# Spreading V by eight one-pass products in 32x128 tiles, with a new order of the work behind them

## The chip, the core and the metric

The kernel runs on one core of a Trainium2 chip. The metric is the device time of one execution in microseconds (us). Five engines work side by side: PE (TensorE, matrix products), DVE (VectorE), ACT (ScalarE), POOL (GpSimd) and SP (SyncE, which here only starts DMAs). Each engine takes its own instructions in the order in which the program lists them, and waits for the others by semaphores.

## The reference

The first half is a scan over sequences (Mamba-2 style, in chunks), the second a mixer of low rank with two dense layers. What matters here:

```python
# x: (4, 8, 768, 32), a: (4, 8, 768), B and C: (4, 8, 768, 16)
for c in range(seq // 32):                       # chunks
    M = (C_c @ B_c.T) * decay(i, j) * causal     # within a chunk
    y_c = M @ x_c + (C_c @ state) * decay_to_i
    state = decay_full * state + (decay_from_j * B_c).T @ x_c
x = y as (4, 768, 256)
h = (x.T @ U) @ V                                # U: (768, 32), V: (32, 768), over the sequence
u = x + h.T
out = u + relu(u @ w_ch1) @ w_ch2                # (256, 1024), (1024, 256)
```

U, V and the weights arrive as float64, so the kernel makes fp32 of them itself.

## The kernel before

**Tiling.** The sequence is worked on in 12 pairs: 4 batches times 3 stretches of 256 positions. For a pair k the steps have one-letter names: P (B and C times decays, DVE, tile `BC`), T (transposes on PE, copies to `T` and `Cm` by ACT), g (`gram`, products of 32x64 tiles into four banks), m and M (`mask`, DVE, tile `M`), s (`state`, PE) and u (`update`, DVE, tile `S`, with POOL making `Sm`), i and j (`inter`, PE, products of `T` and `Sm`), n (`intra`, PE, products of `x` and `M`), y (`yout`, ACT copies to `yT`), t or O (`ytokens`, PE transposes, a copy to `ytok`).

For a batch b the mixer has p (`project`, the product with U, L685), q (`parted`, which makes `ps`, the product p spread over partitions and its remainder), a (`added`, the product of `Vs` and `ps`, L703, that DVE adds to `yT`; two halves j of 384 positions), and then the two layers: for batch 0 U (`plain`, fp32) and for batches 1 to 3 S, f, e, h, J (`split`, `first`, `second`, `third`, `fourth`), which work with operands split into near, far and both parts in fp32r; and d (`down`, the second layer, in pieces, the last of which adds `Vs` times `ps` and sends the output). In PE's program an fp32 product is two MATMULs, each with a weight load of its own; an fp32r product is one.

**Weights.** They come as 32-bit words. `c` (`convert`, `to_fp32`) is called four times for each of 10 pieces: two operations on DVE and one on ACT, one on ACT, two on DVE, one on DVE. c0 and c2 are the first quarter of `w_ch1` (tile `w1f`), c3 to c5 its other quarters, c6 to c9 the quarters of `w_ch2` (tiles `w2c`), c1 is U and V. `R` (`refine`) splits a quarter for the later batches.

**Order.** There is no automatic scheduling: the string `PLAN` lists the steps word by word, and `follow` issues them in that order, so that each engine's program is the part of the plan that falls to it. Words that begin with b, x, B, X, L, w, W, Z, z start loads on SP; a load under B, X, w or L is held until the last DVE operation that was issued before it. F are products of ones that fill time (`warm`). PSUM has 8 banks that go round, the tag `words` has 15 buffers that go round.

**V.** The word v calls `spread` (L818 to L830). V stands in four strips of 32 partitions in `Vq`. ACT makes `Vn`, V in fp32r; DVE writes the remainder over `Vq` (the tile `UV` in the profile). Then PE copies each of the four strips i to all four strips of bank `v[i]`: for q = 0 to 3 a product with a 32x32 piece of the identity, of Vn for even q, of the remainder for odd q. These are 16 fp32 products in 32x32 tiles (L826). ACT copies the banks to `Vs`. The words behind v are `x4.1 b4.1 b4.2 u3.0 u3.1 p0 c2 n3 c0 P4 c0 i3 q0 c2 b5.2 b5.0 T4 T4 j3 y3.0 y3.1 W2 W3 b5.1 W4 a0.0 c2 c2 a0.1 x4.0 w5`.

Of the kernel before, what the change touches and what calls it, by code (L numbers as in the profile page):

```python
# [10 lines left out]
FP32 = mybir.dt.float32  # L11
INT32 = mybir.dt.int32
UINT32 = mybir.dt.uint32
FP32R = mybir.dt.float32r
WCOLS = 512
NWORDS = 15
# [7 lines left out]
ALU = mybir.AluOpType  # L24
# [52 lines left out]


@with_exitstack
def kernel(  # L80
# [27 lines left out]
    nc = tc.nc  # L108
    P = 128
    NB, NH, S, D = x.shape  # L110
    N = B.shape[-1]
    NC = S // P
    NPR = NC // 2
    DM = NH * D
    RK = moe_U.shape[1]
# [7 lines left out]
    Q = 32  # L123
# [3 lines left out]
    const = ctx.enter_context(tc.tile_pool(name="const", bufs=1))  # L127
    raw = ctx.enter_context(tc.tile_pool(name="raw", bufs=4))
    att = ctx.enter_context(tc.tile_pool(name="att", bufs=2))
# [21 lines left out]
    class Kept:  # L151
# [15 lines left out]
    vector = Kept(nc.vector)  # L167
# [7 lines left out]
        out=a_sb,  # L175
# [43 lines left out]
    Vq = UV[:, 1]  # L219
    Vn = const.tile([P, NC * RK], FP32R)  # L220
    Vs = const.tile([P, S], FP32R)
    w1 = [const.tile([P, NCB, DF], FP32R, name=f"w1{i}") for i in range(3)]
    w1all = mix.tile([P, NQ, NCB, W], FP32, tag="u", name="w1f", bufs=1)
    w1f = [w1all[:, c] for c in range(NQ)]
# [28 lines left out]
    own = {}  # L253
# [39 lines left out]
    ident = const.tile([P, P], FP32)  # L293
# [4 lines left out]
    def triangle(name, out, pattern, base, mult, in_=None):  # L298
        nc.gpsimd.affine_select(
            out=out, in_=ones[:, :out.free_size()] if in_ is None else in_, pattern=pattern,  # L300
            compare_op=ALU.is_ge, fill=0.0, base=base, channel_multiplier=mult)
        return out
# [9 lines left out]
    for v in range(2):  # L312
        half = slice(v * H, v * H + H)
        vector.tensor_tensor(out=ref[half, half], in0=upto[half, half],
                                in1=low[v][half, half], op=ALU.subtract)

    same = const.tile([P, Q], FP32)
# [4 lines left out]
    mine = const.tile([P, NH], FP32)  # L322
    triangle("mine", mine, [[-N, NH]], 0, 1)
    triangle("mine", mine, [[N, NH]], N - 1, -1, in_=mine)
    def warm(n, tag="w"):

        idle(bank(tag, 4 * P), n)
# [6 lines left out]
    for g in range(2):  # L334
# [3 lines left out]
        out=la.rearrange("p b c h -> p b h c"),  # L338
        in0=la_ps.rearrange("p g (b h c) -> p (g b) h c", h=NH, c=NC),
        scalar1=1e-6, scalar2=1.0, op0=ALU.max, op1=ALU.min)  # L340
# [17 lines left out]
    for v in range(2):  # L358
        half = slice(v * H, v * H + H)
        vector.tensor_scalar(out=causal[half], in0=upto[half, half], scalar1=-1.0,  # L360
                                scalar2=None, op0=ALU.mult)
# [20 lines left out]
    def keep(bs, tag="w"):  # L382

        n = bs.stop - bs.start
        d = bank(tag, n, NC, 2, NH)
        nc.tensor.matmul(out=d[:, :, :, 0], lhsT=middle, rhs=la[:, bs], start=True, stop=True,
                         skip_group_check=True)
        for m, sl in ((high, slice(0, NC - 1)), (low[0], slice(1, NC))):
            nc.tensor.matmul(out=d[:, :, :NC - 1, 1], lhsT=m, rhs=la[:, bs, sl], start=False,
                             stop=True, skip_group_check=True)  # L390
        J = 2 * NC - 1
        own = att.tile([P, NB, J, NH], FP32, tag="own", name="own", bufs=1)[:, :n]
        vector.tensor_tensor(
            out=own, in0=d.rearrange("p b c v h -> p b (c v) h")[:, :, :J],
            in1=mine[:, None, None, :].to_broadcast(own.shape), op=ALU.mult)
        vector.tensor_reduce(out=kept[:, bs], in_=own, axis=mybir.AxisListType.X, op=ALU.add)
        nc.scalar.activation(kept[:, bs], kept[:, bs], AF.Exp)
        nc.gpsimd.tensor_tensor(
            out=own2[:, bs], in0=kept[:, bs, :, None].to_broadcast([P, n, J, 2]),
            in1=slot[:, None, None, :].to_broadcast([P, n, J, 2]), op=ALU.mult)  # L400
# [417 lines left out]
    def spread():  # L818

        nc.scalar.copy(out=Vn, in_=Vq)  # L820
        vector.tensor_tensor(out=Vq, in0=Vq, in1=Vn.bitcast(FP32), op=ALU.subtract)
        v = [bank(tag, NC * RK) for tag in "yyxz"]
        for q in range(4):
            for i in range(4):
                rows = ts(i, Q)
                nc.tensor.matmul(out=v[i][ts(q, Q)], lhsT=ident[rows, rows],  # L826
                                 rhs=Vq[rows] if q % 2 else Vn[rows].bitcast(FP32),
                                 start=True, stop=True, skip_group_check=True)
        for i in range(4):
            nc.scalar.copy(out=Vs[:, ts(i, NC * RK)], in_=v[i])  # L830

# [23 lines left out]
    def ytokens_kept(k):  # L855
# [9 lines left out]
                 v=lambda n: spread())  # L865
# [51 lines left out]
```

## Time and profile before

| what | us |
|---|---|
| median of 3 runs | 222.32 |
| lowest and highest | 221.99, 222.81 |
| the profiled execution's own time | 222.37 |
| its span in the profile | 220.7 |

The span runs from the first to the last instruction; the profiled execution's own time is 1.67 us longer. The profile has busy times by engine, and lists instructions with engine, line of the kernel, operation, "written <- read" tiles, shapes and counts. For matrix products it gives the tile (rows * columns of the array) ahead of the shape. In brackets stands how long the engine was idle just before, and what ended that; "issue" means nothing that the profile shows. Matmuls overlap, so their durations add up to more than the time from start to start.

### The profile page before, as it was taken

How to read it: one execution, taken by the hardware profiler on the slowest of the kernel's cores; microseconds unless marked ns; L12 is line 12 of the kernel's file. 1: busy time of each engine (PE TensorE's matmuls, PEld its weight loads, DVE VectorE, ACT ScalarE, POOL GpSimd, SP SyncE). 2: the span in 40 equal slices, each digit the busy share in tenths (PEclk: the TensorE clock that was granted, in tenths of full speed). 3: DMA queues.
4: the chain of work that ended last, by engine and by line, in shares of the span. 5: the costliest groups of instructions: out<-in, count | busy, mean ns of one | idle time of the engine just before them, and what ended most of it. 6: DMA issues, size and time to landing. Idle time of an engine off the chain costs nothing.

```text
span 220.7 us, 7036 instructions
## 1 busy us (share of the span) xinstructions
PE 211.9 (96%) x3012; PEld 181.1 (82%) x3012; DVE 154.5 (70%) x330; ACT 114.3 (52%) x261; POOL 15.5 (7%) x37
## 2 busy tenths in 40 slices
PE   7999889999999999999999999999999999999993
PEld 4657565556578789997999899889989999999993
DVE  4786779899985977475298883973847763729832
ACT  2436856857867353765543237246466446366210
POOL 3021010011001300002000210010000000000000
PEclk9999999999999999999999999999999999999999
DMA  6987779778847070000700000200000100020003
GB/s 89 138 118 153 136 120 328 109 164 216 109 59 118 28 98 24 24 3 9 113 27 1 27 18 30 70 11 3 1 3 0 46 28 0 2 70 3 1 27 115
DMA packets 69518, 14.56 MB, mean 66 GB/s; under 512 B 63792, under 2 KB 67696, under 8 KB 69488
## 3 DMA queue, kind: packets, MB, share of 16 engines
q1 hardware_dynamic: 69488, 14.13, 32.4%
q8 instruction: 23, 0.38, 0.7%
q14 instruction: 7, 0.06, 0.1%
HBM read 10.98 MB, written 3.15 MB: 64 GB/s over the span
## 4 chain that ended last, share of the span: by engine, by line
PE 86%; DVE 6%; ACT 3%; issue 2%; DMA 1%; POOL 0%; DVEq 0%; ACTq 0%; POOLq 0%
PE x L731 29%; PE z L731 24%; PE y L731 12%; PE y L642 3%; PE y L620 2%; PE x L516 2%; PE w L485 2%; DVE words L162 2%; PE w L548 2%; PE w L662 2%; PE z L516 1%; PE w L685 1%; DVE M L162 1%; DVE BC L162 1%; PE w L693 1%
## 5 line engine op out<-in xcount | busy, mean ns | idle before, releaser
L162 DVE SCALAR_TENSOR_TENSOR words<-words 128x768 fp32r<-128x768 f32 (+6 forms) x44 | 33.8, 801 | 2.7 <-ACT words L421 1.0
L731 PE MATMUL x<-u,w 128*128 128x384 f32 x144 | 32.4, 344 | 0.0
L731 PE MATMUL z<-u,w 128*128 128x384 f32 x144 | 32.1, 340 | 0.2 <-DVE words L162 0.2
L731 PEld LDWEIGHTS x<-u,w 128*128 128x128 f32 x144 | 24.5, 188 | 0.4 <-issue 0.2
L731 PEld LDWEIGHTS z<-u,w 128*128 128x128 f32 x144 | 24.3, 188 | 0.6 <-issue 0.5
L731 PE MATMUL x<-w2c,words 128*128 128x256 f32 x112 | 23.2, 339 | 0.0
L736 ACT ACTIVATE x<-x 128x384 f32<-128x384 f32 (+1 forms) x30 | 13.7, 456 | 18.3 <-PE x L731 15.4
L162 DVE SCALAR_TENSOR_TENSOR words<-x,words 128x384 fp32r<-128x384 f32 x24 | 13.1, 552 | 12.8 <-ACT words L765 12.6
L162 DVE SCALAR_TENSOR_TENSOR words<-z,words 128x384 fp32r<-128x384 f32 x24 | 13.0, 551 | 12.8 <-ACT words L765 12.8
L731 PE MATMUL y<-w,words 128*128 128x256 f32 x144 | 20.3, 281 | 0.0
L731 PEld LDWEIGHTS x<-w2c,words 128*128 128x128 f32 x112 | 18.4, 189 | 1.4
L731 PEld LDWEIGHTS y<-w,words 128*128 128x128 f32 x144 | 19.3, 189 | 0.2 <-ACT words L765 0.2
L736 ACT ACTIVATE z<-z 128x384 f32<-128x384 f32 (+1 forms) x27 | 12.5, 464 | 13.2 <-PE z L731 13.2
L765 ACT ACTIVATE words<-z 128x384 fp32r<-128x384 f32 x24 | 11.7, 494 | 8.1 <-PE z L731 7.3
L765 ACT ACTIVATE words<-x 128x384 fp32r<-128x384 f32 x24 | 11.2, 490 | 7.1 <-PE x L731 7.1
L576 POOL TENSOR_TENSOR Sm<-S,own 128x256 f32<-128x256 f32 (+1 forms) x12 | 8.6, 721 | 81.8 <-DVE S L162 63.1
L731 PE MATMUL x<-w,words 128*128 128x256 f32 x96 | 14.1, 284 | 0.0
L731 PEld LDWEIGHTS x<-w,words 128*128 128x128 f32 x96 | 12.8, 188 | 0.3 <-issue 0.2
L162 DVE SCALAR_TENSOR_TENSOR S<-S,kept,w 128x64 f32<-128x64 f32 x40 | 11.2, 280 | 2.4 <-PE w L548 0.4
L731 PE MATMUL z<-yT,w1f 128*128 128x384 f32 x32 | 11.8, 496 | 0.0
L731 PE MATMUL x<-yT,w1f 128*128 128x384 f32 x32 | 11.4, 489 | 0.1
L447 ACT ACTIVATE w<-words 128x512 fp32r<-128x512 f32 x8 | 5.0, 628 | 12.5 <-DVE words L162 12.5
(153 smaller groups left out, 398.5 us busy)
## 6 DMA issues: line engine op xcount, KB each, us to landing
words<-in_moe_w_ch_dram SPq DMA_DIRECT2D x7, 512.0 KB, 5.1
x<-in_x_dram SPq DMA_DIRECT2D x24, 128.0 KB, 3.3
out_dram<-ytok SPq DMA_DIRECT2D x24, 128.0 KB, 1.7
bc<-in_B_dram SPq DMA_DIRECT2D x24, 64.0 KB, 3.0
bc<-in_C_dram SPq DMA_DIRECT2D x12, 128.0 KB, 3.2
words<-in_moe_w_ch_dram SPq DMA_DIRECT2D x2, 256.0 KB, 4.1
words<-in_moe_V_dram SPq DMA_DIRECT2D x4, 48.0 KB, 2.6
words<-in_moe_U_dram SPq DMA_DIRECT2D x1, 192.0 KB, 4.1
```

The source lines that it names most:

```text
L162: self.last = call(*args, **kwargs)
L447: nc.scalar.activation(low, far, AF.Copy, scale=1.0 / EPS)
L485: nc.tensor.transpose(out=tp[:, i, v], in_=s["BC"][:, i, c + v].rearrange("p h n -> p (h n)"), identity=ident)
L516: nc.tensor.matmul(out=g[r][cols, c], lhsT=s["T"][rows, 0, c, cols], rhs=s["Cm"][rows, :, :, ts(2 * c + p, Q)].rearrange("r v t i -> r v i ...
L548: nc.tensor.matmul(out=s["A"][p][ts(r, Q), v], lhsT=s["BC"][half, 0, v, 2 * r:2 * r + 2].rearrange("p h n -> p (h n)"), rhs=x_sb[k][half, ...
L576: nc.gpsimd.tensor_tensor(out=s["Sm"][:, sl], in0=s["S"][:, sl].rearrange("p i (s d) -> p i s d", s=2), in1=own2[:, b, 4 * q:4 * q + sl.st ...
L620: product = nc.tensor.matmul(out=y[p][ts(r % 2, H), r // 2, c], lhsT=own[ts(r, Q)], rhs=s["T"][ts(r, Q), 1, :, ts(2 * c + p, Q)].rearrange ...
L642: product = nc.tensor.matmul(out=y[p][ts(i, Q), n, c], lhsT=x_sb[k][half, c, h], rhs=s["M"][half, h // 2, c, h % 2], start=fresh(k, p, [i] ...
L662: nc.tensor.transpose(out=t[:, c, g], in_=yT[b][:, g, ts(2 * q + c, P)], identity=ident)
L731: nc.tensor.matmul(out=t, lhsT=lhsT, rhs=rhs, start=start, stop=True, skip_group_check=True)
L736: nc.scalar.activation(t, t, AF.Copy, scale=1.0 + EPS)
L765: nc.scalar.activation(gs[j, m // 2][0][:, m % 2], t, AF.Relu, scale=NEAR)
```

## The change

The spread takes 8 products instead of 16. A new constant `sides` (32 rows used at a time, 128 columns) holds the identity of 32 twice, at the even strips for half 0 and at the odd strips for half 1. A product with it copies Vn (half 0) or the remainder (half 1) to two strips at once and writes zeros to the other two; the second product adds to the first. All operands are fp32r, and the remainder has a tile of its own, `Vf`. POOL makes `sides` early on. `own`, a scratch tile of `keep`, takes a buffer of the tag `words` now. All words of the plan behind a0.1 stand in a new order, from `x4.0 w5` on.

```diff
...
-    'W2 W3 b5.1 W4 a0.0 c2 c2 a0.1 x4.0 w5 c3 c3 c3 c3 U0.0.0 P5 U0.0.1 U0.1.1 R0 B6 t3 X5 g4 m4 T5 '
-    'M4 T5 c5 c5 U0.1.0 c5 c5 X6 U0.1.3 c4 c4 s4 u4.0 u4.1 w6 w7 w8 U0.0.3 P6 U0.0.2 c6 U0.0.6 s5 c4 '
-    'c4 U0.1.7 c6 U0.1.2 u5.0 u5.1 R0 L8 T6 c7 U0.1.6 c7 U0.1.5 c7 i4 R3 g5 n4 m5 c6 T6 U0.0.5 M5 c8 '
-    'L7 c8 U0.0.4 c8 c9 c7 U0.1.4 U0.0.7 c9 c9 n5 c6 i5 j4 R5 P8 y4.1 y4.0 P7 g6 j5 m6 L10 y5.1 t4 '
+    'W2 W3 b5.1 W4 a0.0 c2 c2 a0.1 x4.0 w5 c3 c3 c3 X5 g4 c4 w8 c3 t3 w6 U0.0.0 m4 c4 U0.0.1 P5 c4 '
+    'c5 U0.1.0 U0.1.1 c5 w7 B6 U0.1.3 T5 M4 U0.1.2 s4 u4.0 c4 n4 u4.1 s5 c6 R1 R0 c5 L7 u5.0 T5 c9 '
+    'u5.1 c7 U0.0.2 c5 c9 c7 U0.1.5 c7 c6 c6 c6 U0.0.3 U0.0.4 U0.1.4 U0.1.6 c8 P6 c8 U0.0.6 c8 '
+    'U0.1.7 c7 d0.1.2.0 c8 c9 i4 g5 m5 T6 c9 d0.1.2.1 d0.1.2.2 T6 L8 M5 d0.1.2.3 U0.0.5 n5 R0 i5 P7 '
...
-    'h3.1.6 d3.1.0.0 d3.1.0.1 d3.1.0.2 d3.1.1.0 d3.1.0.3 d3.1.1.1 J3.1.0 d3.1.1.2 J3.1.1 J3.1.3 '
-    'd3.1.1.3 J3.1.2 d3.1.2.2 d3.1.2.3 d3.0.1.5 d3.1.0.4 d3.1.1.4 d3.0.0.4 d3.1.0.5 d3.1.2.4 '
-    'd3.1.1.5 d3.1.2.5 d3.0.0.5 d3.0.2.4 d3.0.2.5 ')
+    'e3.1.7 h3.1.7 J3.1.3 d3.1.0.0 J3.1.0 d3.1.1.0 d3.0.0.4 h3.1.5 d3.1.2.1 d3.1.2.2 d3.0.0.5 '
+    'd3.1.1.1 d3.1.0.1 d3.1.0.2 d3.1.0.3 d3.1.2.3 J3.1.2 d3.1.1.2 d3.1.1.3 d3.1.0.4 d3.0.2.4 '
+    'd3.1.2.4 d3.1.1.4 d3.0.1.4 d3.1.1.5 d3.1.2.5 d3.0.1.5 d3.0.2.5 d3.1.0.5 ')
...
+    Vf = const.tile([P, NC * RK], FP32R)
...
+    sides = const.tile([P, 2, 4 * Q], FP32R)
+    for half in range(2):
+        both = sides[:, half].rearrange("p (g s r) -> p s g r", g=2, s=2)
+        for s in range(2):
+            nc.gpsimd.tensor_scalar(
+                out=both[:, s], in0=same[:, None, :].to_broadcast([P, 2, Q]),
+                scalar1=float(s == half), scalar2=None, op0=ALU.mult)
...
-        own = att.tile([P, NB, J, NH], FP32, tag="own", name="own", bufs=1)[:, :n]
+        own = raw.tile([P, 2 * WCOLS], INT32, tag="words", name="words", bufs=NWORDS).bitcast(
+            FP32)[:, :n * J * NH].rearrange("p (b j h) -> p b j h", b=n, h=NH)
...
-        vector.tensor_tensor(out=Vq, in0=Vq, in1=Vn.bitcast(FP32), op=ALU.subtract)
+        vector.tensor_tensor(out=Vf, in0=Vq, in1=Vn.bitcast(FP32), op=ALU.subtract)
         v = [bank(tag, NC * RK) for tag in "yyxz"]
-        for q in range(4):
+        for half, part in enumerate((Vn, Vf)):
             for i in range(4):
                 rows = ts(i, Q)
-                nc.tensor.matmul(out=v[i][ts(q, Q)], lhsT=ident[rows, rows],
-                                 rhs=Vq[rows] if q % 2 else Vn[rows].bitcast(FP32),
-                                 start=True, stop=True, skip_group_check=True)
+                nc.tensor.matmul(out=v[i], lhsT=sides[rows, half], rhs=part[rows],
+                                 start=half == 0, stop=True, skip_group_check=True)
```

56 rows, old and new, of the table PLAN are left out of this document.

## The prediction

> **What bounds the kernel now.** I read the page first, then busy time by stage, then the timeline where the change begins. The page's rows are busy time, granted clock by fortieths, and the chain that ended last by engine:
>
> ```profile
> PE 211.9 (96%) x3012; PEld 181.1 (82%) x3012; DVE 154.5 (70%) x330; ACT 114.3 (52%) x261; POOL 15.5 (7%) x37
> PEclk9999999999999999999999999999999999999999
> PE 86%; DVE 6%; ACT 3%; issue 2%; DMA 1%; POOL 0%; DVEq 0%; ACTq 0%; POOLq 0%
> ```
>
> TensorE (PE) is the bound, at the full clock throughout, and the chain is 86% PE. A busy PE can hide waits, so I look at it by stage (columns: length, then busy us and count of PE, weight loads, DVE, ACT, POOL; clock, DMA share, GB/s):
>
> ```profile
> 28.75:40.00 11.25, 10.62 (x177) 6.88 (x168) 9.90 (x24) 7.75 (x20) 0.95 (x2) 1.00 0.90 229
> 40.00:62.00 22.00, 22.00 (x345) 13.35 (x352) 19.78 (x43) 17.10 (x35) 2.70 (x4) 1.00 0.82 152
> 62.00:100.00 38.00, 37.84 (x613) 32.80 (x599) 28.24 (x60) 20.87 (x46) 3.70 (x7) 1.00 0.27 47
> 100.00:217.00 117.00, 116.82 (x1285) 111.58 (x1283) 76.26 (x138) 55.01 (x126) 3.47 (x7) 1.00 0.10 26
> ```
>
> From 28.75 us on, all that the change reorders, PE is idle for 0.63 + 0 + 0.16 + 0.18 = 0.97 us. A new order of the same work cannot win much more than that from waits. DVE is close behind PE up to 62 us (19.78 of 22.00 us), and far behind it later.
>
> **The spread of V.** This is where the 16 products run, with what stands before and behind them:
>
> ```profile
> 27.14 0.35 PE L826 MATMUL y<-Vn,ident 32*32 32x192 f32 x2
> 27.28 0.35 DVE L162 TENSOR_TENSOR UV<-UV,Vn 128x192 f32<-128x192 f32 x1
> 27.34 0.32 PE L826 MATMUL x<-Vn,ident 32*32 32x192 f32 x1
> ...
> 28.23 0.34 PE L826 MATMUL z<-Vn,ident 32*32 32x192 f32 x1 [0.57 <-issue]
> ...
> 28.50 0.32 PE L826 MATMUL z<-UV,ident 32*32 32x192 f32 x1
> 28.75 0.86 PE L685 MATMUL x<-ytok,UV 128*32 128x256 f32 x16
> 28.91 0.54 ACT L830 CAST Vs<-y 128x192 fp32r<-128x192 f32 x2 [1.82 <-PE z L826]
> ```
>
> Each fp32 product is two MATMULs. Seven of the 32 start by 27.34; then PE stands until 28.23, and the other 25 start within 0.27 us. So of the 1.61 us from the first product to the next work (L685), 0.89 us is a hole between two passes of one product, which no data can explain: the profile calls it "issue". The same word stands twice before it, and I counted what PE did between the holes:
>
> ```profile
> 19.15 0.36 PE L548 MATMUL w<-x,BC 64*32 64x64 f32 x18 [0.27 <-issue]
> 23.15 0.45 PE L642 MATMUL y<-M,x 64*32 64x64 f32 x30 [0.66 <-issue]
> ```
>
> ```profile
> 19.15:23.15 4.00, 3.34 (x127) 2.79 (x127) 3.15 (x10) 2.51 (x7) 0.51 (x1) 1.00 0.66 124
> 23.15:28.23 5.08, 4.23 (x127) 2.76 (x127) 4.26 (x13) 3.59 (x9) 0.18 (x1) 1.00 0.77 137
> ```
>
> ```profile
> q8 instruction: 23, 0.38, 0.7%
> ```
>
> Each time it is 127 matmuls and 127 weight loads, 254 instructions, from hole to hole, and the instruction queue moves 0.38 MB in 23 pieces, 16 KB each. PE waits for the next piece of its own program, at a time when the data DMAs are at 0.66 to 0.77. So I read the hole as one at a fixed place in PE's instruction list, not as one of the spread. Everything ahead of the spread is the same in both programs on PE, so the hole comes behind the same 14 instructions. Before, these are 7 of 32 passes; after, 7 of the 8 one-pass products. Only the eighth is left at 28.23.
>
> [...]
>
> What one product of the new form costs, no row shows (32x128 tile, 192 columns, one pass). The nearest rows bound it: the old passes start some 0.01 us apart (25 in 0.27 us), and full-width one-pass products of 256 columns take 12.76 / 106 = 0.12 us each:
>
> ```profile
> 204.27 12.76 PE y L731 x106
> ```
>
> So 8 take 0.1 to 1.0 us, and I take the dear end, 0.12 each, since the new tiles span all columns. The first four need Vn alone: done by 27.14 + 0.48 = 27.62. The others need Vf from DVE: 27.28 + 0.35 = 27.63, as before. Three end by 28.0, hidden by the hole, and the eighth ends at 28.23 + 0.12 = 28.35. L685 starts there, not at 28.75: **0.40 us** earlier. Bounds: 0 (the piece of program comes later by so much) and 28.75 - 28.17 = 0.58 (no hole: 27.63 + 0.06 + 0.48 = 28.17).
>
> Is it kept? These rows follow:
>
> ```profile
> 30.23 0.68 DVE L162 TENSOR_TENSOR BC<-bc,F 128x512 f32<-128x512 f32 x1
> 31.28 0.60 PE L485 MATMUL w<-ident,BC 128*128 128x128 f32 x4
> 31.48 0.37 ACT L695 CAST ps<-w 128x256 fp32r<-128x256 f32 x1 [0.97 <-PE w L693]
> 31.89 0.43 DVE L162 TENSOR_TENSOR ps<-w,ps 64x256 fp32r<-64x256 f32 x1 [0.64 <-ACT ps L695]
> 32.37 0.45 PE L703 MATMUL x<-Vs,ps 128*128 128x384 f32 x1
> 32.85 0.56 DVE L162 TENSOR_TENSOR yT<-x,yT 128x384 f32<-128x384 f32 x1 [0.54 <-PE x L703]
> ```
>
> Here PE, ACT and DVE wait for each other in turn, and ACT and DVE stand idle before their parts (0.97, 0.64, 0.54), so an earlier PE moves all of it. PE's transposes at 31.28 need BC, ready at 30.91, and can go 0.37 earlier. So all but 0.03 of the 0.40 is kept.
>
> **The rest of the first part.** The subtraction writes Vf, not Vq: the same 0.35 us. Four multiplications for `sides` on POOL, and `own` in a buffer of words:
>
> ```profile
> 3.37 0.19 POOL L299 TENSOR_SCALAR_AFFINE_SELECT mine<-mine 128x8 f32<-128x8 f32 x1
> 9.84 0.37 POOL L398 TENSOR_TENSOR own<-kept,slot 128x88 f32<-128x88 f32 x1 [6.28 <-ACT kept L397]
> ```
>
> POOL idles 6.28 us just where they stand; even at 0.5 us each they cost nothing. If that cover were gone, `own2` would come up to 2 us later (4 x 0.5), and the first Sm behind it. `own` takes a buffer 15 allocations ahead of its next use: nothing.
>
> **The new order.** DVE and ACT issue the same instructions; on PE only their neighbours differ. What neighbours cost:
>
> ```profile
> 149.96 0.86 PE L731 MATMUL z<-u,w 128*128 128x384 f32 x4
> 150.66 0.86 PE L731 MATMUL x<-u,w 128*128 128x384 f32 x4
> 151.44 0.78 PE L620 MATMUL y<-T,Sm 32*64 32x64 f32 x32
> ```
>
> Four products take 0.70 us when products of the same tile follow (149.96 to 150.66), and 0.78 when tiles of 32x64 follow: 0.08 us for a change of tile shape. Counted in the two orders, PE changes shape 70 times before and 66 times after: 4 x 0.08 = **0.3 us** less. Bounds: 0 and, if leaving costs as much again, 0.6.
>
> [...]
>
> Waits: of the 0.97 us of idle PE, some go and some come. I take the sum as unchanged, **0**, since both orders leave DVE and PE about as near to each other at most places; bounds are -0.97 and the DVE rival's +1.65 below. SP issues two loads of x behind an output now, and w2's last quarter ahead of the others; all are due tens of us later.
>
> **The tail.** One product, one addition, one output as before:
>
> ```profile
> 214.22 3.61 SPq L802 DMA_DIRECT2D out_dram<-ytok  x5
> 217.05 0.42 DVE L162 TENSOR_TENSOR ytok<-y,ytok 128x256 f32<-128x256 f32 x1 [0.64 <-PE y L731]
> ```
>
> After, the last five outputs follow at 5 products each, 0.6 us apart; five already go in 3.61 us. Nothing.
>
> **Sum.** The profiled execution took 222.37 us (span 220.7 and 1.67 around it), 0.05 over the median of 222.32. 222.37 - 0.40 - 0.30 = 221.67; on the median's scale **221.6 us**.
>
> **Rivals.**
>
> *DVE sets the pace up to 62 us (slower).* In the new order weights are wanted sooner. From the first addition of V p to the last quarter of w2, DVE has 27.7 us of work and PE 28.1 us before it needs that quarter; before it was 31.6 against 36.7 (counted in the two orders with the mean step of each form). DVE starts 0.48 us behind PE there (32.37 and 32.85 above). The 5 us of reserve are gone. DVE's waits on ACT in this stretch before were:
>
> ```profile
> 42.05 1.31 DVE L162 SCALAR_TENSOR_TENSOR words<-words 128x512 f32<-128x512 f32 x2 [0.71 <-ACT words L421]
> 57.69 1.30 DVE L162 SCALAR_TENSOR_TENSOR words<-words 128x512 f32<-128x512 f32 x2 [0.26 <-ACT words L421]
> 61.54 0.69 DVE L162 SCALAR_TENSOR_TENSOR words<-words 128x512 int32<-128x512 int32 x1 [0.68 <-ACT words L423]
> ```
>
> 0.71 + 0.26 + 0.68 = 1.65 us. If they all come back, PE waits that long, at the down products that read the new quarter: 223.3. Should ACT's conversion steps queue behind relus that wait for PE, one more wait of 0.7 gives 224.0. It is slower than before from 0.7 us of such waits on. For it: the reserve. Against it: ACT is wanted later than DVE in most of the new places, and PE has a wait of its own after the second addition that gives DVE some back. 0.20.
>
> *The waits go (faster).* Between the two additions and the next work PE now has gram and transposes of pairs 4 and 3, where it waited for DVE before; if most of the 0.97 us goes: 220.7 to 221.0. 0.27 for below 221.2.
>
> *The hole goes with the 32 passes.* If it is no wait for a piece of program, L685 starts at 28.17 and the gain there is 0.58: 222.32 - 0.58 - 0.30 = 221.4. For it: the hole lies in a burst of small passes, which are now few. Against it: 254 instructions twice. 0.05. [...]
>
> *The spread gives nothing.* The piece of program comes 0.4 us later, or the hole moves into L685, and its successor at 256 instructions on falls into the next gram: 222.0. 0.13.
>
> **Chances.** Forecast, 221.2 to 221.9: 0.35. About 0.5% (1.1 us) is what a measurement can tell from no change, so faster means below 221.2, slower above 223.4. Faster 0.27. Slower 0.10, half of the DVE rival; its other half lies between 222 and 223.4. Same: 0.35 + 0.05 + 0.13 + 0.10 = 0.63. Range 220.6 to 223.2: it takes in the vanished waits and the DVE rival at most of its price.
>
> **What would show it.** Right: in the timeline a single product of the spread at 28.2 behind "issue", L685 at 28.3 to 28.4, L703 at 32.0, and the same distance to the end less 0.3. Wrong: L685 at 28.7 or later; weight loads or matmuls of the first down products idle on "DVE w2c" or "DVE w1f" between 45 and 62; PE busy in 40 to 62 clearly below its length.

## The result, and the profile after

| | before | after |
|---|---|---|
| median, us (12 runs each, side by side) | 222.26 | 220.50 |
| lowest and highest | 221.36, 225.49 | 219.56, 221.83 |
| the profiled execution's own time | 222.37 | 220.41 |
| its span | 220.7 | 218.7 |

The ratio of the mean times is 0.9913, with a 95% interval from 0.9885 to 0.994; by the medians it is 1.8 us faster. The forecast was 221.6 with a range from 220.6 to 223.2, so the time lies 0.1 us below the range. That margin is smaller than the scatter of the runs; what has to be explained is why the gain is more than twice the forecast's 0.7. On two other chips the changed kernel had 0.9903 and 0.9925 (e11 and e16 below). In the runs below, executions over 1.5% longer than the fastest of their kernel are left out of the ratio (in e9 two of four).

The page after: busy time, granted clock by fortieths, the chain that ended last.

```profile
PE 210.3 (96%) x2988; PEld 182.4 (83%) x2988; DVE 154.0 (70%) x330; ACT 114.2 (52%) x261; POOL 17.7 (8%) x41
PEclk9999999999999999999999999999999999999999
PE 83%; DVE 11%; issue 2%; ACT 1%; DMA 1%; POOL 0%; DVEq 0%; POOLq 0%; ACTq 0%
```

PE is still the bound; DVE's share of the chain has grown from 6 to 11%. By stage (length, then busy us and count of PE, weight loads, DVE, ACT, POOL; clock, DMA share, GB/s):

```profile
28.75:40.00 11.25, 11.04 (x166) 7.19 (x159) 10.30 (x26) 8.44 (x21) 1.15 (x2) 1.00 0.98 239
40.00:62.00 22.00, 21.30 (x237) 13.89 (x236) 20.58 (x45) 14.23 (x30) 3.49 (x3) 1.00 0.56 120
62.00:100.00 38.00, 37.81 (x573) 32.60 (x579) 24.89 (x55) 22.25 (x49) 2.60 (x5) 1.00 0.40 65
100.00:215.00 115.00, 115.00 (x1431) 111.38 (x1424) 77.96 (x140) 55.25 (x127) 4.01 (x8) 1.00 0.10 25
```

PE's idle column sums to 0.21 + 0.70 + 0.19 + 0 = 1.10 us behind 28.75; before it was 0.97. By this column no wait was won. Yet from the first product behind the spread to the last product of the program there were 216.73 - 28.75 = 187.98 us before, and there are now 214.73 - 28.58 = 186.15:

```profile
27.49 0.35 PE L835 MATMUL y<-Vn,sides 32*128 32x192 f32 x2
...
28.04 0.36 PE L835 MATMUL y<-Vf,sides 32*128 32x192 f32 x2 [0.19 <-DVE Vf L162]
...
28.30 0.35 PE L835 MATMUL z<-Vf,sides 32*128 32x192 f32 x1
...
28.58 0.86 PE L694 MATMUL x<-ytok,UV 128*32 128x256 f32 x16
```

```profile
214.73 0.28 PE L740 MATMUL y<-ps,Vs 128*128 128x256 f32 x1
```

and of before:

```profile
216.73 0.28 PE L731 MATMUL y<-ps,Vs 128*128 128x256 f32 x1
```

The spread itself went from 28.75 - 27.14 = 1.61 us to 28.58 - 27.49 = 1.09. Of the 1.09, some 0.5 is the wait for `Vf` and some 0.25 the hole ahead of the eighth product. The spread began 0.35 us later in this execution than in the one of before, with the same code ahead of it on PE; that start lies between 26.3 and 27.9 us in the executions below in which nothing is added ahead of it. So 0.35 - 0.52 - 1.83 = -2.0, the difference of the spans. One new wait stands between 58 and 61 us, the one which the prediction's slower rival had named:

```profile
58.87 0.38 PE L494 MATMUL w<-ident,BC 128*128 128x128 f32 x2
59.95 1.13 PE L740 MATMUL x<-w2c,words 128*128 128x256 f32 x4 [0.70 <-DVE w2c L162]
```

In the chain of waits (start, us, what) DVE is the link for most of 43.57 to 59.91 there; its end:

```profile
56.23 1.20 DVE w2c L162 x2
57.43 1.20 DVE words L162 x2
58.63 0.67 DVE M L162 x2
59.30 0.61 DVE w2c L162
```

Two things are thus to be explained: where 1.83 us came from when the idle column shows no gain, and what part the spread and the order have in it.

One measure is used throughout: the time from one product's start to the next one's, against the same step (tile shapes, widths, types) elsewhere in all traces. An fp32 product counts as one step, with both its passes. What a step is too long is called its excess. PE's ends in the profile are modelled, and its idle column shows a wait only beyond the modelled end of the product ahead of it; the step has all of it (0.54 us at 102.6 us of e1, where the column has 0.19).

### The profile page after: what moved, and what is told of

Same layout as the page of the kernel before. It is cut to its first block, busy times and chain, and to the rows that moved or that the text cites. A ratio compares the mean times of both kernels' runs of the same rounds, so it can differ in the third digit from the quotient of the medians.

```text
span 218.7 us, 6992 instructions
## 1 busy us (share of the span) xinstructions
PE 210.3 (96%) x2988; PEld 182.4 (83%) x2988; DVE 154.0 (70%) x330; ACT 114.2 (52%) x261; POOL 17.7 (8%) x41
## 4 chain that ended last, share of the span: by engine, by line
PE 83%; DVE 11%; issue 2%; ACT 1%; DMA 1%; POOL 0%; DVEq 0%; POOLq 0%; ACTq 0%
PE x L740 27%; PE z L740 22%; PE y L740 12%; DVE words L162 5%; PE y L651 3%; PE y L629 3%; PE x L525 2%; PE w L671 2%; DVE M L162 2%; PE w L494 2%; DVE S L162 2%; PE w L557 1%; PE z L525 1%; PE w L694 1%; DMA a_sb<-in_a_dram 1%
## 5 line engine op out<-in xcount | busy, mean ns | idle before, releaser
L740 PE MATMUL x<-u,w 128*128 128x384 f32 x144 | 32.1, 342 | 0.0
L740 PE MATMUL z<-u,w 128*128 128x384 f32 x144 | 32.1, 342 | 0.0
L740 PEld LDWEIGHTS x<-u,w 128*128 128x128 f32 x144 | 24.6, 188 | 0.4 <-issue 0.2
L740 PEld LDWEIGHTS z<-u,w 128*128 128x128 f32 x144 | 24.3, 188 | 0.4 <-issue 0.2
L740 PE MATMUL x<-w2c,words 128*128 128x256 f32 x112 | 22.8, 339 | 0.7 <-DVE w2c L162 0.7
L740 PE MATMUL y<-w,words 128*128 128x256 f32 x144 | 20.3, 280 | 0.0
L740 PEld LDWEIGHTS x<-w2c,words 128*128 128x128 f32 x112 | 18.2, 189 | 2.4 <-DVE w2c L162 0.9
L740 PEld LDWEIGHTS y<-w,words 128*128 128x128 f32 x144 | 19.2, 188 | 0.0
L740 PE MATMUL x<-w,words 128*128 128x256 f32 x96 | 14.3, 285 | 0.0
L585 POOL TENSOR_TENSOR Sm<-S,own 128x256 f32<-128x256 f32 (+1 forms) x12 | 8.1, 676 | 76.3 <-DVE S L162 44.7
L740 PEld LDWEIGHTS x<-w,words 128*128 128x128 f32 x96 | 12.9, 189 | 0.1
L740 PE MATMUL z<-w2c,words 128*128 128x256 f32 x56 | 11.5, 339 | 0.2 <-DVE S L162 0.2
L651 PE MATMUL y<-M,x 64*32 64x64 f32 x768 | 10.5, 225 | 1.0 <-issue 0.9
L663 ACT COPY yT<-y 128x256 f32<-128x256 f32 x24 | 7.8, 380 | 6.9 <-PE y L629 6.9
```

What stands on the lines that cost most here:

```text
L585: nc.gpsimd.tensor_tensor(out=s["Sm"][:, sl], in0=s["S"][:, sl].rearrange("p i (s d) -> p i s d", s=2), in1=own2[:, b, 4 * q:4 * q + sl.st ...
L651: product = nc.tensor.matmul(out=y[p][ts(i, Q), n, c], lhsT=x_sb[k][half, c, h], rhs=s["M"][half, h // 2, c, h % 2], start=fresh(k, p, [i] ...
L663: nc.scalar.copy(out=yp[:, :, :, p], in_=st[k]["y"][p])
L740: nc.tensor.matmul(out=t, lhsT=lhsT, rhs=rhs, start=start, stop=True, skip_group_check=True)
```

## The experiments

"Distance" is from the first product behind the spread to the last one of the program, in the profiled execution.

| run | median us | ratio to before, 95% | distance us |
|---|---|---|---|
| after | 220.50 | 0.9913 [0.9885, 0.994] | 186.15 |
| e1 new spread, old order | 222.16 | 0.9981 [0.995, 1.0012] | 188.10 |
| e2 old spread, new order | 223.58 | 1.0048 [1.0018, 1.0079] | 190.06 |
| e3 new order to 62 us, then old | 221.84 | 0.997 [0.9938, 1.0001] | 188.02 |
| e4 old order to 62 us, then new | 223.04 | 1.0023 [0.9997, 1.0049] | 189.00 |
| e5 after, two moves near 59 us | 221.01 | 0.9933 [0.9909, 0.9958] | 189.55 |
| e6 after, 48 more PE instructions | 223.53 | 1.0042 [1.0012, 1.0072] | 189.43 |
| e7 e2 and 208 more | 226.33 | 1.014 [1.0103, 1.0178] | 189.55 |
| e8 after and 256 more | 226.85 | 1.0203 [1.016, 1.0245] | 188.69 |
| e9 as e7, in four places | 228.26 | 1.0154 [1.0081, 1.0226] | 187.71 |
| e10 after, two passes a product | 220.34 | 0.9883 [0.9847, 0.9919] | 186.18 |
| e11 after again | 221.11 | 0.9903 [0.9866, 0.9939] | 186.05 |
| e12 e5 again | 221.09 | 0.9932 [0.9899, 0.9964] | 186.71 |
| e13 e1, one wait moved away | 221.45 | 0.997 [0.9936, 1.0005] | 187.88 |
| e14 e1, two waits moved away | 220.04 | 0.9925 [0.9896, 0.9954] | 187.10 |
| e15 e1, four waits moved at | 221.46 | 0.9927 [0.9898, 0.9955] | 187.52 |
| e16 after beside e15 | 221.24 | 0.9925 [0.9892, 0.9957] | 187.36 |

### The parts alone (e1 to e4)

The theory was that spread and order add up. e1 is the changed kernel with the plan of before, e2 the kernel of before with the new plan; e3 and e4 are the changed kernel with the plan cut near 62 us (behind d0.1.2.3 of the new one, and at the same point of the old):

```diff
 # e1, on the changed kernel
-... a0.1 x4.0 w5 c3 c3 c3 X5 g4 c4 w8 c3 t3 w6 U0.0.0 ...
+... a0.1 x4.0 w5 c3 c3 c3 c3 U0.0.0 P5 U0.0.1 U0.1.1 ...
 # e2, on the kernel of before: the same line the other way round
```

> The new spread of V (with sides, Vf and own's new buffer), the whole old order. Theory: the spread gives 0.4 to 0.5 us by itself, since only its last product is left behind the hole in PE's program, and nothing else moves: 221.8 against 222.3. Rival (the spread gives nothing, because the products of POOL at the start or the hole take it back): 222.3. Second rival (the spread's 0.5 us grow, because waits behind it shrink too): below 221.2.

> The old spread of 16 products, the new order. Theory: all but the spread's 0.5 us of the change comes from the order, some 1.3 us: 221.0. Rival (spread and order work only together, since the order was made for the earlier L685): 221.8 or more.

> The new spread, the new order up to the fourth piece of the first down product (62 us in its trace), and what is left in the old order. Theory, by the excess of PE's steps in the two traces: up to 62 us the new order wins 0.8 us of waits at 31 to 40 and loses 0.8 at 59 (the last quarter of w2 comes late), so this kernel has the spread's gain alone: 221.8. Rival (fewer changes of tile shape and waits gain evenly along the way): 221.3.

> The new spread, the old order up to the last step of the last conversion (62 us), and what is left in the new order. Theory: the order's gain lies behind 62 us (waits at 63 to 80 and at 102.7 us that the new order doesn't have, and 0.3 us of tile changes): 220.5, as fast as the whole change. Rival (even along the way): 221.0 to 221.3.

e1 came out as expected in its median (222.16 beside 222.62 of before), but its interval takes in no change. The profiles are clearer: from the spread's first product to the last product of the program e1 takes 188.94 us, before 189.59. e2 did not come out as expected: the order alone is slower than before. Three steps of its trace hold the loss:

```profile
81.18 0.29 PE L620 MATMUL y<-T,Sm 32*64 32x64 f32 x2 [0.88 <-issue]
...
103.47 0.66 PE L485 MATMUL w<-ident,BC 128*128 128x128 f32 x4 [1.55 <-issue]
...
152.85 0.39 PE L731 MATMUL x<-w,words 128*128 128x256 f32 x1 [0.84 <-PE z L731]
```

Their excesses are 1.16, 1.61 and 1.01 us, 3.8 in all; 190.06 less that is 186.3, about the distance of the changed kernel (186.15). The first two are the hole of the prediction, PE waiting for nothing but its program, now in bursts of 32x64 products. The third carries another name in the bracket, the product ahead of it, and has the same cause, as the next runs show. Nothing stops PE at these three places of the plan in the changed kernel, which differs there only in what lies far ahead: 48 instructions fewer in the spread (32 passes of two instructions before, 8 after).

e3 and e4 settle nothing: each seam of the two plans brings waits of its own, on POOL in e3 and on w2c in e4, where the old first half has not made the last quarter when the new second half wants it. So neither half's share of the gain follows from them.

```profile
102.48 0.60 PE L629 MATMUL y<-T,Sm 32*64 32x64 f32 x16 [0.49 <-POOL settled L592]
```

```profile
63.14 1.10 PE L740 MATMUL x<-w2c,words 128*128 128x256 f32 x4 [1.12 <-DVE w2c L162]
```

### The ends of the program's blocks (e6 to e9, e10)

New theory: PE's program comes in blocks of 256 instructions; where a block ends in a burst of tiny products, PE is through its rest before the next one is there. 48 instructions more or fewer move every end behind them. Rival: the old spread costs the new order something else. All four kernels add tiny products, which nobody reads, to the filler ahead of the spread (e9: to four fillers); 12 products are 48 instructions.

```diff
-    def warm(n, tag="w"):
-        idle(bank(tag, 4 * P), n)
+    def warm(n, tag="w", tiny=0):
+        t = bank(tag, 4 * P)
+        idle(t, n)
+        for i in range(tiny):
+            nc.tensor.matmul(out=t[:Q, 3 * P:3 * P + 16], lhsT=one[:Q].to_broadcast([Q, Q]),
+                             rhs=one[:Q].to_broadcast([Q, 16]), start=True, stop=True,
+                             skip_group_check=True)
```

> The changed kernel, with 12 fp32 products of 32 rows, 32 columns of weights and 16 columns of data added to the filler ahead of the spread (48 instructions on PE, into a part of the bank that nobody reads): the number by which the old spread is longer than the new one, so that all the code behind it lies as in the run with the new order alone. Theory (PE's program comes in blocks of 256 instructions, and where a boundary falls in a burst of tiny products PE waits for the next block): PE stops with 'issue' ahead of it near 80 us (in a burst of L629), near 102 us (L629 to L494) and near 151 us, 0.9 to 1.6 us each, as with the order alone; with 24 passes of some 16 ns, 0.4 us, for the products themselves the time is 220.5 + 0.4 + 3.1 = 224.0. Rival (the old spread costs its own time in the new order, not its length in instructions): no such stops, 220.9.

> The new order alone (the spread of before), with 52 such products, 208 instructions, added to the same filler: with the 48 of the old spread that makes 256, one whole block, so that the code behind the spread lies against the blocks as in the changed kernel. Theory of the blocks: the stops near 80, 102 and 151 us are gone; 104 passes of some 16 ns cost 1.7 us, and perhaps a stop of some 1 us comes in the filler itself: 223.6 - 3.3 + 1.7 = 222.0, up to 223.0; from the spread's first product to the last product of the program 187.5 instead of 191.2. Rival (the stops belong to the order with this spread, not to where blocks end): stops stay, 225.3, and 191.2 from spread to end.

> The changed kernel with 64 such products, 256 instructions, in the same filler: one whole block more, so that the code behind lies as in the changed kernel. The control to the two others: theory of the blocks: no stop near 80, 102 and 151 us, 187.2 us from the spread's first product to the last product of the program, and 220.5 + 2.0 for the added products (128 passes of 16 ns), up to 1.3 more for a stop among them: 222.5 to 223.8. Rival (any lengthening of the program ahead of the spread disturbs what follows): over 188.5 from spread to end.

> The new order alone (the spread of before) with 208 more instructions on PE ahead of the spread as in the run before, but as four groups of 13 tiny products behind four fillers (near 9, 13, 16 and 27 us), not as one run of 3.2 us, behind which PE's clock was granted at 0.50. Theory of the blocks: no stop near 80, 102 and 151 us; no half clock behind the spread; from the spread's first product to the last product of the program 187.4 us (the changed kernel 187.2, the order alone 191.2). With 104 passes of 31 ns, 3.2 us, of which up to 1 lies in waits, the whole is 223.6 - 3.8 + 2.2 to 3.2 = 222.0 to 223.0. Rival (the old spread itself costs the new order its gain): 190.5 to 191.2 from spread to end, 226 in all.

e6 is the plain answer. The changed kernel with 48 instructions more has e2's time (223.53 and 223.58) and e2's three stops, at the same products (L633, L498, L744 here are L620, L485, L731 there):

```profile
82.03 0.27 PE L633 MATMUL y<-T,Sm 32*64 32x64 f32 x1 [0.88 <-issue]
...
104.30 0.60 PE L498 MATMUL w<-ident,BC 128*128 128x128 f32 x4 [1.60 <-issue]
...
153.08 1.10 PE L744 MATMUL x<-w,words 128*128 128x256 f32 x8 [0.42 <-PE z L744]
```

e7, e8 and e9 add up to whole blocks, and none of them stops there. From the first down product that reads w2c (all of e2's three stops lie behind it) to the last product it takes 159.80 us in the changed kernel, 163.81 in e2 and 163.17 in e6, but 160.05, 160.49 and 160.33 in e7, e8 and e9. So from there on the new order keeps its gain with the old spread too, once the ends lie where they do in the changed kernel.

The whole times of e7 to e9 were missed by far, for three reasons that the traces show. A tiny product's step is 79 ns (52 from 26.27 to 30.29 us in e7, one stop among them), where 32 had been reckoned: the 16 ns a pass of the forecasts were the author's estimate, and no run shows them. Blocks also end in bursts elsewhere: in e9 at 20.8 and 25.9 us (excess 1.72 and 0.73), at the end of the spread (1.00) and at 37.4 us (0.95). And behind some 4 us of tiny products, in e7 and e8 PE's clock was granted at half for 10.2 and 6.8 us; e7's windows (PE busy, granted clock, DMA share, GB/s):

```profile
30.00:32.00 2.00, 1.92 (x56) 0.71 0.66 128
32.00:34.00 2.00, 2.00 (x82) 0.50 0.95 349
34.00:36.00 2.00, 2.00 (x20) 0.50 1.14 337
36.00:38.00 2.00, 2.00 (x18) 0.50 0.55 115
38.00:42.00 4.00, 4.00 (x43) 0.62 0.02 4
```

e9's four runs scatter from 225.48 to 230.47, and its profile is of the fastest. That one was granted 0.999 of the clock on average, the others 0.977 to 0.992, so half clock is part of the scatter; the rest stays open.

The strongest evidence lies across all runs. I counted in each program the place of the first instruction behind every excess of over 0.25 us later than 15 us (its place within blocks of 256, where PE's matmuls, weight loads and semaphore instructions count). In the 18 traces 45 of them stand at place 193, 194, 195 or 196 of 256. None of the waits on data named in this document stands there; theirs are other places, which move against the blocks from kernel to kernel. The hole of the prediction (28.23 before, 28.30 after) is one of the 45. From the moment at which a block's transfer starts on the instruction queue to the first instruction behind its end it took 2.0 to 3.1 us in these 45, of which the transfer itself 0.9 to 1.8. Most ends bring no such stop: of 23 in the trace of before three do (19.15, 23.15 and 28.23 us), of 23 after two (23.50 and 28.30). At the ends of these two traces without one, later than 15 us, the same time was 2.28 us or more. So I read a stop as a burst that was through the rest of its block before the next one was there. An end in a burst is not enough: two in the changed kernel, at 100.40 (L651) and 104.44 us (L629), show steps of 0.05 us at most.

e10 asks what the one pass is worth: the eight products read as fp32, two passes each.

```diff
-                nc.tensor.matmul(out=v[i], lhsT=sides[rows, half], rhs=part[rows],
+                nc.tensor.matmul(out=v[i], lhsT=sides[rows, half].bitcast(FP32),
+                                 rhs=part[rows].bitcast(FP32),
```

> The changed kernel, whose 8 products of the spread read the same tiles as fp32, two passes each: the 32x128 tiles without the one pass. 8 more passes, 16 more instructions. If the spread's worth lies in the hole in PE's program that ended 0.3 to 0.6 us behind its start, and in what follows, and not in its passes: 8 passes of 20 to 50 ns, 220.5 + 0.2 to 0.4 = 220.8. Rival (16 instructions already move an end of a block into a burst): a stop of 0.5 to 1.7 us behind 40 us, 221.5 to 222.5.

220.34, 186.18 us of distance, and 28.47 - 27.26 = 1.21 us for the spread against 1.09: the one pass is worth some 0.1 us, within the noise of the whole. 16 more instructions brought no stop, where 48 more brought three (e6): for the work behind the spread, what counts is where the ends come to lie.

### The wait at 59 us (e5, e11, e12)

```diff
-g5 m5 T6 c9 d0.1.2.1 d0.1.2.2 T6 L8 M5 d0.1.2.3 U0.0.5
+g5 c9 m5 T6 d0.1.2.1 d0.1.2.2 T6 L8 M5 U0.0.5 d0.1.2.3
```

> The changed kernel with two moves in its order, between 56 and 62 us: the transposes of the second c9 (L494) stand ahead of m5 and T6, and U0.0.5 (a first product, ready long before) ahead of d0.1.2.3. In the changed kernel's trace PE goes from those transposes to the first down product L740 with 0.87 us more than that step takes elsewhere, while the last quarter of w2 is still being written by DVE. Theory (that wait is on PE's path, and DVE has slack behind it): it goes, and the time is 220.5 - 0.8 = 219.7. Rival (DVE sets the pace there, and the wait only comes a little later, at the next product that reads w2c or words): 220.3 to 220.6.

> The changed kernel again, beside the others on the same chip: 220.5, ratio 0.991; 187.2 us from the spread's first product to the last product, and no stop of PE with 'issue' ahead of it behind 30 us.

> The order with two moves between 56 and 62 us again, beside the changed kernel on the same chip, since the profiled execution of its first run held a late transfer at 30 us (PE idle 1.84 us on DVE's BC, DVE 1.71 on the load of bc) and a half clock behind it. Theory (the wait of 0.87 us at 59 us is PE's own and goes): 0.6 to 0.9 us under the changed kernel. Rival (DVE sets the pace there; the wait moves to the next product that needs it): within 0.4 us of it, and waits on DVE of some 0.8 us in all between 58 and 68 us.

e5's profiled execution was its slowest (223.0): a load of B came late, and DVE and PE behind it.

```profile
31.55 0.69 DVE L162 TENSOR_TENSOR BC<-bc,F 128x512 f32<-128x512 f32 x1 [1.71 <-DMA bc<-in_B_dram]
...
32.30 0.55 PE L494 MATMUL w<-ident,BC 128*128 128x128 f32 x3 [1.84 <-DVE BC L162]
```

So it was run again beside the changed kernel: 221.09 and 221.11. My theory fell. The wait on w2c is gone, and two others have come that make up for it:

```profile
59.64 1.56 PE L740 MATMUL z<-yT,w1f 128*128 128x384 f32 x4 [0.50 <-DVE M L162]
...
66.28 0.44 PE L494 MATMUL w<-ident,BC 128*128 128x128 f32 x2 [0.27 <-DVE M L162]
```

Between 43 and 60 us DVE sets the pace in the new order (see the chain of waits above); these two moves of PE's work only chose which product waits.

### The waits of the old order (e13 to e16)

Where does the order's gain sit? The largest excesses of the old order (e1's trace), and what the idle column shows at the same place:

| step begins at us, step onto | excess us | idle column us (gaps under 0.15 are not listed) |
|---|---|---|
| 30.3 transposes of BC (L494) | 0.57 | 0.3, DVE BC |
| 38.7 transposes of BC (L494) | 0.48 | 0.41, ACT ytok |
| 63.7 transposes of BC (L494) | 0.31 | none |
| 79.3 second addition of V p (L712), two steps | 0.28 + 0.16 | none |
| 102.6 first products (L740) | 0.54 | 0.19, DVE words |

In the changed kernel the first of them is 0.32 (0 in e11) and the others are gone; 0.87 at 59 us and 0.35 at 71 us are new. e13 to e15 take such waits out of the old order by moves of PE's work alone:

```diff
 # e13, on e1
-h1.0.6 L9 f1.1.1 f1.1.5 d0.1.2.3
+h1.0.6 d0.1.2.3 L9 f1.1.1 f1.1.5
 # e14, on e13
-t3 X5 g4 m4 T5 M4 T5 c5 c5 U0.1.0 c5 c5
+t3 X5 g4 m4 c5 c5 U0.1.0 T5 M4 T5 c5 c5
 # e15, on e14
-t4 d0.1.0.0 T8 y5.0 d0.1.0.1 T8
+t4 d0.1.0.0 y5.0 d0.1.0.1 T8 T8
-R3 P10 q1 d0.0.0.0 R6
+R3 P10 d0.0.0.0 q1 R6
```

> The new spread with the old order, and one move in it: d0.1.2.3, two down products whose data is long ready, stands ahead of f1.1.1 instead of two places behind it. In the run with the new spread alone the step onto f1.1.1's first product (102.6 us) takes 0.54 us more than such a step takes elsewhere, while PE's idle column shows 0.19 us there ('DVE words'). Theory (the step tells the wait, the idle column only its uncovered end): from the spread's last product to the last product of the program 188.10 - 0.4 to 0.5 = 187.65. Rival (the idle column tells it): 187.9.

> That move, and a second one near 39 us: U0.1.0, two first products, stands ahead of T5, whose transposes (L494) wait there for ACT to empty their bank (step 0.48 us longer than elsewhere, idle column 0.41). Theory (the order's gain is a sum of such waits, each worth its step): 188.10 - 0.95 = 187.15 from the spread's last product to the last product, and 0.4 to 0.5% under the new spread alone in time, 221.2 to 221.8 where that had 222.2. Rival (each wait comes back at the next product that needs DVE or ACT, and the order's gain has another source): within 0.2 us of 188.1.

> Two more moves in the old order with the new spread: d0.1.0.1, two down products, ahead of T8, whose transposes wait near 63 us for ACT to empty the bank (step 0.31 us longer than elsewhere), and d0.0.0.0 ahead of q1, the second addition of V p, whose products wait near 79 us on DVE (steps 0.28 and 0.16 longer). Theory (each wait is worth its step): 187.10 - 0.31 - 0.3 to 0.44 = 186.35 to 186.5 from the spread's last product to the last product, about what the whole new order reaches (186.05 to 186.18), and 0.2 to 0.35% under the run with two moves. Rival (they come back at the next product): 187.0.

> The changed kernel on the same chip as the run with four moves: 220.5, ratio 0.991; 186.1 us from the spread's last product to the last product.

e14 lands on the theory: 187.10 against 187.15 forecast, and 188.1 for the rival. In e1 the two places look like this,

```profile
39.43 0.63 PE L494 MATMUL w<-ident,BC 128*128 128x128 f32 x4 [0.41 <-ACT ytok L676]
...
103.34 0.94 PE L740 MATMUL z<-u,w 128*128 128x384 f32 x4 [0.19 <-DVE words L162]
```

and in e14 the brackets are gone:

```profile
38.43 1.56 PE L740 MATMUL x<-yT,w1f 128*128 128x384 f32 x4
39.82 0.60 PE L494 MATMUL w<-ident,BC 128*128 128x128 f32 x4
...
103.08 0.68 PE L740 MATMUL z<-u,w 128*128 128x384 f32 x3
```

The idle column gave these two 0.60 us; taking them away won 188.10 - 187.10 = 1.00. e13's 187.88 is the rival's 187.9, but it holds a stop of 0.33 at 147.3 us at place 194 of a block; without it the distance would be 187.55, on the theory's side. e14, an old order with two moves, can't be told from the new one by its ratio: 0.9925 against 0.9913, 0.9903 and 0.9925. By distance it is still 0.95 longer than the changed kernel.

e15 is half a miss. The wait at 63 us went and did not come back. That ahead of L712 did not go, because the second move was the wrong way round: q1 is not the addition but makes `ps`, which the addition a1.0 (L712) reads. With d0.0.0.0 ahead of q1, one product piece less stands between q1 and a1.0, and the first product of L712 starts 0.44 us behind the pass ahead of it, where it was 0.16 in e14. The weight loads of e15 name both waits:

```profile
79.19 0.19 PEld L712 LDWEIGHTS x<-Vs,ps 128*128 128x128 f32 x1 [0.46 <-DVE ps L162]
79.65 0.19 PEld L712 LDWEIGHTS z<-Vs,ps 128*128 128x128 f32 x1 [0.27 <-DVE M L162]
```

The first is the one that the move lengthened. The second, the wait that it was meant to take away, stands in e1 and e14 with the same 0.27: DVE is making `M` from a bank z there, and the product writes a bank z. Neither is a wait for PE's own work, and no run moved the mask. A stop of 0.38 at 147.6 us, at place 195 of a block, took the rest: 187.10 - 0.31 + 0.28 + 0.38 = 187.45, where 187.52 was measured. No old order was run that beats the changed kernel. e16's distance is longer than the changed kernel's other two for one reason, a half clock near 30 us:

```profile
28.00:30.00 2.00, 1.72 (x20) 0.65 0.81 104
30.00:32.00 2.00, 2.00 (x81) 0.50 0.71 70
```

## Why the prediction was wrong, point by point

**The spread, -0.40: right.** -0.52 in the profile, by the mechanism named: four products, three more when `Vf` is there, the eighth behind the end of a block at 28.30. The terms were coarser than they looked: from the spread's first product to L694 the same eight took 0.84 (e1, where the eighth starts at 28.05 with the three ahead of it), 1.09 and 1.36 us (e11); that the block came early or late is my reading. "Is it kept?": e1 keeps 0.65 of the 0.77 that its spread is shorter, in one execution each; by its ratio, 0.9981, it can't be told from no change.

**Sides and own, 0: right.** POOL's four multiplications took 1.48 us from 3.51 on, and no row waits for them.

**Change of tile shape, -0.30: not contradicted.** The steps of some 0.08 us at a change of shape are still the same size (from a pass of `u,w` to a product of 32x64 tiles 0.26 us at 151.44 before and at 151.61 after, where the step to a further such pass is some 0.175), and between 130 and 160 us the trace shows four changes fewer, 8 for 12. No run had this alone.

**Waits of the order, 0: this is the step that failed.** "A new order of the same work cannot win much more than that from waits", 0.97 us, was read off the idle column. That column leaves out the part of a wait that lies under the modelled end of the product ahead. Five places of the old order are worth 2.3 us by their steps, and two of them, 0.60 by the column, gave 1.00 when taken away (e14). The new order removes most of the 2.3 and adds 0.87 and 0.35. From e1 to the changed kernel, with the same spread, the distance falls by 188.10 - 186.15 = 1.95, where the forecast had 0.30 for the order: some 0.8 is the balance of those waits. The other 1.15 lies in many small steps, changes of shape among them, and its cause stays open. Counted pass by pass, against the step between two passes of one kind, steps that are 0.06 to 0.14 us too long fall from 66 to 54 where a small tile stands on one side (1.1 us) and from 25 to 19 between full-width products (0.6 us), while those of 0.03 to 0.06 at small tiles rise from 44 to 59 (0.6 us).

**The DVE rival, 223.3: its place was right, its price was not.** PE waits at the product named, 0.87 us by the step instead of 1.65, and e12 shows that DVE sets the pace there. I had given it as the slower end; it was outweighed.

**"The waits go", 220.7 to 221.0 at 0.27** is nearest to what happened. Its price had the same bound from the idle column, which is why the range ended too high.

**The tail, 0: right.** From the last product to the end of the span 220.7 - 216.73 = 3.97 us before, 218.7 - 214.73 = 3.97 after.

**What the prediction did not see at all:** that spread and order don't add. The blocks' ends were used for one hole at 28 us, and "its successor at 256 instructions on" got half a sentence. But the 48 instructions that the spread saves move 18 ends behind it. In the old order they are worth little (e1: 0.46 us in the medians); in the new order 223.53 - 220.50 = 3.0 us, and by the distance, in which the added products have no part, 189.43 - 186.15 = 3.3. With the old spread the new order is slower than before (e2). That in the changed kernel none of the 18 ends behind the spread stops PE for 0.25 us or more was no part of the forecast: that it came out faster at all rests on this, and as far as the forecast goes it was luck.

## What to carry to other kernels

Count PE's instructions in long straight code: here 48 more or fewer moved every block's end behind them, and a burst of tiny products that came to lie across an end stopped PE for up to 1.7 us (e9), so an order is only as good as the length of the code ahead of it. Read waits of PE from start to start against the same step elsewhere, not from the idle column (1.00 us won in e14 where the column had 0.60). When work is added to shift or delay something, look at the granted clock behind it before the time is read (0.50 for 10.2 us in e7).

## What the runs showed that was not expected

- A stop at a block's end can carry a product's name in the bracket instead of "issue" (0.84 us `<-PE z L731` in e2, 0.42 `<-PE z L744` in e6): the place in the program tells it from a wait, the bracket doesn't.
- PE's clock fell to 0.50 for 10.2 and 6.8 us behind 52 and 64 products of 32x32 tiles and 16 columns (e7, e8), though the profile calls PE busy there (2.00 of 2.00 us in each window from 32 to 38); 12 of them did not do it (e6). It also fell in e16 near 30 us, and in e5 behind the idle 1.84 us, for 3.4 us each. What brings it on was not shown.
- Single steps can mislead where an fp32r product follows an fp32 one of 256 columns. At 105.6 us before, it starts 0.03 us behind the last fp32 pass, where the fp32 passes ahead of it start 0.22 behind each other, and the product behind it comes 0.19 us later than usual (0.31 instead of 0.12). The two cancel, so such a pair has to be read as one.
